# Hash attention with a squared-ReLU feed-forward block: the layout of the first pair's loads, and the parts in which the next chunk's x is loaded

## The chip, the cores and the metric

The kernel runs on one core of one Trainium2 chip. The metric is device microseconds (us) of one execution on that core. The core has a matrix engine (TensorE, PE in the profile; its weight loads are shown apart as PEld), a vector engine (VectorE, DVE), a scalar engine (ScalarE, ACT), GpSimd (POOL) and SyncE (SP). SP, ACT and POOL also issue DMA transfers, each in its own program order; sixteen DMA engines carry them out.

## The reference

Attention over 4 x 8 heads of 768 tokens with 64 features. Six sign bits of a projection give each query and each key a bucket, and a query attends only to keys of its own bucket. The result, 3072 tokens by 512, goes through a feed-forward block with a squared ReLU.

```
q_bits = (einsum('bhsd,dk->bhsk', q, proj) > 0)      # the same for k
mask = q_bucket[:, :, :, None] == k_bucket[:, :, None, :]
scores = where(mask, q @ k.T / sqrt(D), -1e9)
attn = softmax(scores) @ v                           # (4, 8, 768, 64)
x = attn.transpose(0, 2, 1, 3).reshape(3072, 512)
h = x @ w_in                                         # (3072, 2048)
out = (maximum(h, 0) ** 2) @ w_out                   # (3072, 512)
```

## The kernel before, in words

The work of every engine is written out by hand: inside `tc.manual_schedule()` each engine, and each queue of DMA issues, runs its instructions in the order in which the program names them. An instruction that waits holds back all that stands behind it on its engine.

**Attention** (lines 598 to 693, 0 to about 331 us) goes over 16 pairs of heads. For pairs 1 to 15 `load_pair` brings q and k in blocks that VectorE can transpose (`features`). The first pair has a path of its own. `load_first` (L267) loads q and k with six consecutive tokens on one partition, so each partition takes one run of 1536 B per head; one head goes through SP's queue and one through ACT's. `keep_busy(6)` (L329) puts six products of no use on PE while the loads are under way. `first_features(w, r)` (L306) turns three blocks of 128 tokens: per block and head, a product of the loaded 128 x 64 block with the identity gives 64 x 128 in PSUM (L314). The result is copied to `feat`: for q (w = 0) with a strided copy that puts the tokens in their order again, on ScalarE for r = 0 and on VectorE for r = 1 (L319); for k (w = 1) in the order in which it lies, on VectorE (L324). The values of the first pair are loaded with the same six tokens on a partition (L298), so that keys and values agree; later pairs load them in rows of 256 B (L300). Then come the hash products (L352), the signs (L362 on ScalarE, L376 and L380 on VectorE), the scores (L402) and their exponentials (L419). The attention result goes to a DRAM tensor, `x_all`, features by tokens (L503).

**The feed-forward block** (lines 1217 to 1252) goes over three chunks of 1024 tokens. For each chunk there is a stage of hidden products and then `project(i)` (L1059), which makes the output by seven products of blocks, k = 0 to 6, each of them split into seven again. One of these, `product` (L708), runs seven `add` steps of eight PE instructions each on L717, with factors of w_out ("leaf") that ACT's queue loads ahead. In the middle of its program stands `hook` (L1135). Its first instruction is a subtraction on VectorE, `minus(y21, y21, t2)`; the result is the moving operand `t4` of the last `add` of the same product. So the last eight PE instructions of each k wait for that subtraction. After it come `inner_sums(k + 1)`, the sums for the next product.

While chunk 0 is projected, each of k = 0 to 3 begins with `factor_units(k)` (L838). It builds factors of w_in that the next chunk needs: two loads through POOL's queue (L842, 256 KB each), four sums on VectorE (L516 to L519), and four stores through POOL's queue (L851), two of which wait for the sums. Its tiles `h` come from a ring of five buffers.

`load_x(i)` (L557) loads chunk i of `x_all`, 2 MB, through POOL's queue into one tile of four feature blocks. For the next chunk it is called after product k = 0 (L1155). The first reader is `sum_x` on VectorE after product k = 3 (L1157).

The main function is one long function; here is what the diff touches:

Of the kernel before, what the change touches and what calls it, by code (L numbers as in the profile page):

```python
# [8 lines left out]
FP32 = mybir.dt.float32  # L9
# [25 lines left out]
def kernel(  # L35
# [17 lines left out]
    P = 128  # L53
# [212 lines left out]

    def load_first():  # L267


        for src, name in ((q, "q_nat"), (k, "k_nat")):  # L270
            t = p_qk.tile([P, 2, SB, D], FP32, name=name)
            for h, queue in enumerate((nc.sync, nc.scalar)):
                queue.dma_start(
                    out=t[:, h], in_=src[0, h].rearrange("(p t) d -> p t d", t=SB)
                )
            nat[0, name] = t
        for h, queue in enumerate((nc.sync, nc.scalar)):
            queue.dma_start(out=projs[h * D:(h + 1) * D, 0:NBITS], in_=proj)
# [15 lines left out]
    def load_values(pr):  # L294
        b, j = divmod(pr, PB)
        t = p_v.tile([P, 2, SB * D], FP32, name="v_nat")
        if pr == 0:
            nc.sync.dma_start(out=t, in_=v[0, 0:2].rearrange("h (p t) d -> p h (t d)", t=SB))  # L298
        else:
            nc.sync.dma_start(  # L300
                out=t.rearrange("p h (t d) -> p (h t) d", d=D),
                in_=v[b, 2 * j:2 * j + 2].rearrange("h (t p) d -> p (h t) d", t=SB),
            )
        nat[pr, "v_nat"] = t

    def first_features(w, r):  # L306

        if r == 0:
            feat[0, w] = p_f.tile([P, S], FP32, name=f"feat{w}")
        tp = turn("tp")[:, 0]  # L310
        for i in range(SB // 2):
            t = r * (SB // 2) + i
            for h in range(2):
                nc.tensor.matmul(  # L314
                    out=tp[h * D:(h + 1) * D, i * P:(i + 1) * P],
                    lhsT=nat[0, ("q_nat", "k_nat")[w]][:, h, t], rhs=ident, start=True, stop=True,
                )
        if w == 0:
            (nc.vector.tensor_copy if r else nc.scalar.copy)(  # L319
                out=feat[0, w].rearrange("f (p t) -> f t p", t=SB)[:, r * (SB // 2):(r + 1) * (SB // 2)],  # L320
                in_=tp[:, 0:HS].rearrange("f (t p) -> f t p", p=P),
            )
        else:
            nc.vector.tensor_copy(out=feat[0, w][:, r * HS:(r + 1) * HS], in_=tp[:, 0:HS])  # L324

    busy = const.tile([P, 512], BF16, name="busy")
    void = ps_o.tile([P, 1024], FP32, name="xo")
# [1 line left out]
    def keep_busy(n, w=512):  # L329

        for _ in range(n):
            nc.tensor.matmul(  # L332
                out=void[:, 0:w], lhsT=busy[:, 0:P], rhs=busy[:, 0:w], start=True, stop=True
            )
# [186 lines left out]
    def minus(out, in0, in1):  # L521
        nc.vector.tensor_tensor(out=out, in0=in0, in1=in1, op=ALU.subtract)  # L522
# [31 lines left out]

    xs = {}

    def load_x(i):  # L557

        x = p_c.tile([P, NFT, NCH], FP32, name="x")
        nc.gpsimd.dma_start(out=x, in_=x_all[:, :, i * NCH:(i + 1) * NCH])  # L560
        xs[i] = x, [p_c.tile([P, 2, NCH // 2], FP32, name=f"t_x{n}") for n in range(3)]

    w_unit = {}

# [33 lines left out]
    with tc.manual_schedule():  # L598
        nc.vector.memset(busy, 1.0)
        nc.vector.memset(projs, 0.0)  # L600
        load_first()
        keep_busy(6)
        make_identity(nc, ident)
        constants()
        load_pair(1)
# [2 lines left out]
            load_weight(i)  # L608
        first_features(0, 0)
        first_features(0, 1)  # L610
        first_features(1, 0)
        hash_bits(0, void.rearrange("p (h c) -> p h c", h=2), (0,))
        signs(0, 0)
# [445 lines left out]
        def project(i):  # L1059

            V, W, U, X = (p_y.tile([P, 4, QN], FP32, name=f"sum{n}") for n in range(4))
            outs = {}

            def out_block(ih, jh, n):

                row, col = n // 2, n % 2
                if (ih, jh, row) not in outs:
                    outs[ih, jh, row] = [p_y.tile([P, HN], FP32, name="o", bufs=NOUT), 0]
                o = outs[ih, jh, row]
                return o[0][:, col * QN:(col + 1) * QN]  # L1070

            def close(ih, jh, n):
                o = outs[ih, jh, n // 2]
                o[1] += 1
                if (i, ih, jh, n // 2) == (NCHUNK - 1, 1, 0, 1):

                    if o[1] == 2:
                        for col in (1, 0):
                            put_last(n - n % 2 + col, o[0][:, col * QN:(col + 1) * QN])
                elif o[1] == 2:  # L1080
                    put_out(i, ih, jh, n // 2, o[0])

            def first_(n, one, two):
                if two is None:
                    nc.scalar.copy(out=block(V, n), in_=one)
                else:
                    add_to(block(V, n), one, two)

            def seventh(n, one, two):
                add_to(block(W, n), block(V, n), whole(one, two))  # L1090

            def fifth(n, one, two):
                if two is None:
                    nc.scalar.copy(out=block(U, n), in_=one)
                else:
                    add_to(block(U, n), one, two)

            def third(n, one, two):
                add_to(block(X, n), block(U, n), whole(one, two))
                add_to(block(X, n), block(X, n), block(V, n))  # L1100

            def second(n, one, two):
                add_to(out_block(0, 0, n), block(V, n), whole(one, two))
                close(0, 0, n)

            def sixth(n, one, two):
                t = whole(one, two)
                add_to(out_block(0, 1, n), block(X, n), t)
                close(0, 1, n)
                add_to(block(W, n), block(W, n), t)  # L1110
                add_to(out_block(1, 1, n), block(W, n), block(U, n))
                close(1, 1, n)

            def fourth(n, one, two):
                add_to(out_block(1, 0, n), block(W, n), whole(one, two))
                close(1, 0, n)

            more = i + 1 < NCHUNK
            uses = first_, seventh, fifth, third, second, sixth, fourth
            for k in range(7):  # L1120
                b = OUTER[k][1]
                t1, t2 = tens.pop(k)
                if i == 0 and k < NQ:
                    factor_units(k)
                if k == 6 and more:
                    load_inner(i + 1, 0)
                at = lambda m, k=k: lambda n: leaves[k, m][:, n]
                bt = {
                    "11": lambda n: b[:, n, 0:QN], "21": lambda n: b[:, NQ + n, 0:QN],
                    "22": lambda n: b[:, NQ + n, QN:HN], "t1": lambda n: t1[:, n],  # L1130
                    "t2": lambda n: t2[:, n], "t3": lambda n: b[:, n, QN:HN],
                    "t4": lambda n: b[:, NQ + n, 0:QN],
                }

                def hook():  # L1135
                    y21 = b[:, NQ:NR, 0:QN]
                    minus(y21, y21, t2)
                    if k + 1 < 7 and k not in (1, 3):
                        inner_sums(k + 1)
                    if k == 6 and more:  # L1140
                        sums_inner(i + 1)

                counted = []

                def a_with_load(m, k=k):
                    load_leaf(7 * k + len(counted) + NLEAF - 2)
                    counted.append(m)
                    return at(m)

                use = uses[k]  # L1150
                product(
                    NQ, QN, a_with_load, bt, lambda *p: use(0, *p), lambda *p: use(1, *p),
                    lambda p: use(2, p, None), lambda *p: use(3, *p), hook,
                )
                if k == 0 and i + 1 < NCHUNK:  # L1155
                    load_x(i + 1)
                if k in (3, 4) and i + 1 < NCHUNK:  # L1157
                    sum_x(i + 1, 2 * k - 5)
                    sum_x(i + 1, 2 * k - 4)
                if k == 5 and i + 1 == NCHUNK:  # L1160
                    guard()
                if k == 0:

                    for h in range(2):
                        at_h = slice(h * NQ, (h + 1) * NQ)
                        minus(b11[:, at_h], b22[:, at_h], b_t[:, at_h])
                    inner_sums(2)
                if k == 2:

                    for h in range(2):  # L1170
                        at_h = slice(h * NQ, (h + 1) * NQ)
                        minus(b_t[:, at_h], b21[:, at_h], b11[:, at_h])
                    inner_sums(4)
# [315 lines left out]
```

## Time and profile before

| what | value |
|---|---|
| median of 3 runs | 880.36 us (879.87 to 880.45) |
| the profiled execution's own time | 880.36 us |
| its span in the profile | 878.5 us |
| PE busy | 865.6 us, 99% of the span |
| VectorE busy | 760.8 us, 87% |
| ScalarE busy | 391.7 us, 45% |
| POOL busy | 106.9 us, 12% |
| granted TensorE clock, mean | 0.997 |
| x loads (L560) | 3 of 2 MB, median 11.9 us from issue to landing |

The profile is one execution. The span runs from the first to the last instruction, and 1.9 us of the time lie outside it. Busy times count an engine's own instructions; a DMA is counted with the queue that issued it. The chain of work that ended last is followed back from the last instruction: 96% of it is PE. A timeline shows the instructions of an engine in order, "x8" being eight of one kind merged; square brackets hold the idle time before them and what ended it, as far as the profile can tell. "issue" there means that the profile found no releaser.

### The profile page before, as it was taken

The numbers are of one execution on the slowest core, as the hardware profiler recorded it, in microseconds if no ns is written. First come the engines' busy times: TensorE is split into PE (matmuls) and PEld (weight loads), VectorE is DVE, ScalarE is ACT, GpSimd is POOL, SyncE is SP. The second block draws the span as 40 slices with busy tenths as digits, with TensorE's granted clock in tenths as the row PEclk, the third lists the DMA queues.
The fourth block names the chain that finished last, engine by engine and source line by source line (L and its number), as shares of the span: only waits on it lengthen the run. The fifth ranks groups of instructions, "written<-read, shape, count | busy, mean of one in ns | idle before, by whom it ended". The sixth has DMA issues, their size and how long they took to land.

```text
span 878.5 us, 12193 instructions
## 1 busy us (share of the span) xinstructions
PE 865.6 (99%) x4372; PEld 521.1 (59%) x4372; DVE 760.8 (87%) x1100; ACT 391.7 (45%) x672; POOL 106.9 (12%) x172
## 2 busy tenths in 40 slices
PE   8999999999999999999999999999999999999996
PEld 4444444444444444444688865556888755568885
DVE  5999999999999998888779968888889788888875
ACT  6988888888888852222211123332111233321110
POOL 2000000000000000554231011111000211110002
PEclk9999999999999999999999999999999999999998
DMA  9676987899888636999897764536857744455565
GB/s 195 119 150 127 240 164 148 183 257 220 178 183 217 161 108 213 297 263 287 295 342 249 179 159 171 168 117 224 287 147 189 169 162 156 127 167 152 160 171 109
DMA packets 220291, 167.09 MB, mean 190 GB/s; under 512 B 159840, under 2 KB 177504, under 8 KB 220224
## 3 DMA queue, kind: packets, MB, share of 16 engines
q1 hardware_dynamic: 186592, 87.19, 41.3%
q0 software_dynamic: 12528, 41.30, 15.1%
q10 hardware_dynamic: 21104, 37.76, 14.2%
q8 instruction: 36, 0.59, 0.3%
q14 instruction: 31, 0.25, 0.1%
HBM read 124.52 MB, written 41.68 MB: 189 GB/s over the span
## 4 chain that ended last, share of the span: by engine, by line
PE 96%; DVE 2%; ACT 1%; issue 0%; DVEq 0%; ACTq 0%
PE acc L717 40%; PE st L402 17%; PE acc L936 16%; PE xo L444 14%; PE acc L889 6%; PE hash L352 2%; PE tot L461 1%; DVE total L434 1%; ACT bits L362 1%; PE tp L314 0%; ACT e L419 0%; PE xo L332 0%; PE xo L483 0%; DVE x_t L499 0%; DVE recs L493 0%
## 5 line engine op out<-in xcount | busy, mean ns | idle before, releaser
L419 ACT ACTIVATE e<-st 128x1024 f32<-128x1024 f32 x192 | 145.1, 810 | 44.9 <-PE st L402 41.1
L402 PE MATMUL st<-feat,feat 64*128 64x512 f32 (+1 forms) x768 | 150.4, 483 | 0.0
L444 PE MATMUL xo<-e,v_nat 128*64 128x512 f32 (+1 forms) x768 | 134.8, 492 | 0.0
L717 PE MATMUL acc<-b,leaf 128*128 128x256 f32 x600 | 133.4, 379 | 0.9 <-issue 0.9
L717 PEld LDWEIGHTS acc<-b,leaf 128*128 128x128 f32 x600 | 113.8, 190 | 17.6 <-issue 2.3
L434 DVE TENSOR_TENSOR total<-total,e 128x1536 f32<-128x1536 f32 x64 | 112.4, 1756 | 8.2 <-ACT e L419 3.6
L444 PEld LDWEIGHTS xo<-e,v_nat 128*64 128x64 f32 x768 | 51.3, 136 | 82.1 <-issue 74.0
L936 PE MATMUL acc<-t_x,w_unit 128*128 128x512 f32 x192 | 90.2, 592 | 0.0
L402 PEld LDWEIGHTS st<-feat,feat 64*128 64x128 f32 x768 | 66.0, 188 | 32.7 <-issue 23.4
L717 PE MATMUL acc<-t,leaf 128*128 128x256 f32 x336 | 76.2, 380 | 0.0
L362 ACT ACTIVATE bits<-hash,lifts 32x384 bf16<-32x384 f32 x120 | 68.7, 573 | 2.3 <-PE hash L352 0.4
L717 PEld LDWEIGHTS acc<-t,leaf 128*128 128x128 f32 x336 | 63.7, 190 | 9.1 <-DVE t L522 0.5
L801 DVE SCALAR_TENSOR_TENSOR b<-h 128x512 f32<-128x512 f32 x96 | 65.7, 691 | 3.0
L402 PE MATMUL st<-bits,bits 64*128 64x256 bf16 (+1 forms) x384 | 63.0, 325 | 1.7 <-ACT e L419 1.3
L936 PE MATMUL acc<-x,w_unit 128*128 128x512 f32 x128 | 60.2, 592 | 0.0
L717 PE MATMUL acc<-x,w_unit 128*128 128x512 f32 x128 | 56.5, 593 | 0.0
L717 PE MATMUL acc<-b_t,leaf 128*128 128x256 f32 x240 | 53.8, 379 | 0.0
L936 PEld LDWEIGHTS acc<-t_x,w_unit 128*128 128x128 f32 x192 | 36.5, 190 | 28.9 <-issue 26.8
L724 ACT COPY two<-acc 128x256 f32<-128x256 f32 (+1 forms) x29 | 12.5, 432 | 87.7 <-PE acc L717 72.2
L724 ACT COPY one<-acc 128x256 f32<-128x256 f32 (+1 forms) x29 | 12.5, 432 | 85.6 <-PE acc L717 52.1
L717 PEld LDWEIGHTS acc<-b_t,leaf 128*128 128x128 f32 x240 | 45.5, 190 | 6.2
L402 PEld LDWEIGHTS <-bits 64*128 64x128 bf16 x384 | 23.6, 93 | 42.5 <-issue 38.3
(160 smaller groups left out, 1169.7 us busy)
## 6 DMA issues: line engine op xcount, KB each, us to landing
leaf<-w_out ACTq DMA_DIRECT2D x142, 256.0 KB, 3.1
w_unit<-w_in SPq DMA_DIRECT2D x16, 640.0 KB, 4.0
raw<-in_moe_w_in_dram SPq DMA_DIRECT2D x16, 512.0 KB, 5.5
raw<-in_moe_w_out_dram SPq DMA_DIRECT2D x16, 512.0 KB, 4.5
w_unit<-w_in SPq DMA_DIRECT2D x8, 896.0 KB, 7.7
w_out<-sums POOLq DMA_DIRECT2D x16, 448.0 KB, 6.8
sum<-w_in SPq DMA_DIRECT2D x16, 448.0 KB, 4.9
v_nat<-in_v_dram SPq DMA_DIRECT2D x16, 384.0 KB, 4.4
```

The source lines that it names most:

```text
L352: nc.tensor.matmul(out=banks[g * NR_B:(g + 1) * NR_B, h, 0:HS], lhsT=projs[rows], rhs=feat[pr, w][rows, c * HS:(c + 1) * HS], start=True, ...
L362: nc.scalar.activation(out=t[h * D:h * D + NR_B, c * HS:(c + 1) * HS], in_=hashed[pr, w][at, h, 0:HS], func=ACTF.Sign, scale=HUGE, bias=li ...
L402: nc.tensor.matmul(out=st[:, h, 0:hi - lo], lhsT=src[pr, 1][rows, key], rhs=src[pr, 0][rows, lo:hi], start=first, stop=not first,)
L419: nc.scalar.activation(out=e[:, :, lo:hi], in_=sts[i][:, :, 0:hi - lo], func=ACTF.Exp, scale=scale)
L434: nc.vector.tensor_tensor(out=totals[pr], in0=totals[pr], in1=weights[pr, kt][:, :, 0:S], op=ALU.add)
L444: nc.tensor.matmul(out=xo[h * D:(h + 1) * D, lo:hi], lhsT=nat[pr, "v_nat"][:, h, kt * D:(kt + 1) * D], rhs=weights[pr, kt][:, h, lo:hi], s ...
L461: nc.tensor.matmul(out=tot[g * 32:(g + 1) * 32, 0:HS], lhsT=ones, rhs=totals[pr][:, h, c * HS:(c + 1) * HS], start=True, stop=True,)
L717: nc.tensor.matmul(out=acc[to], lhsT=a(i), rhs=b(i), start=first and i == 0, stop=last and i == n - 1, skip_group_check=True,)
L724: nc.scalar.copy(out=t, in_=acc[of])
L801: nc.vector.scalar_tensor_tensor(out=out, in0=h, scalar=0.0, in1=h, op0=ALU.max, op1=ALU.mult)
L889: nc.tensor.matmul(out=out, lhsT=w[:, a], rhs=b, start=start, stop=stop, skip_group_check=True)
L936: nc.tensor.matmul(out=acc[to], lhsT=w[:, PLACE[a], f], rhs=bt[b](f), start=first and f == 0, stop=last and f == NFT // 2 - 1, skip_group_ ...
```

## The change

Two separate edits, at the two ends of the kernel's program.

The first pair's path: q, k and v of pair 0 are loaded with token t x 128 + p on partition p, in rows of 256 B. `first_features` turns a block of 128 tokens and both heads with one 128 x 128 transposing product. All of its copies to `feat` run without a stride; both halves of q are copied by ScalarE. Eight products of no use stand ahead of q's blocks, and two more between q's blocks and k's.

The next chunk's x: `load_x` takes a range of feature blocks. Block 0 is loaded in the hook of product k = 0, block 1 after that product, block 2 in the hook of k = 1 and block 3 after it; each is 512 KB.

```diff
-            t = p_qk.tile([P, 2, SB, D], FP32, name=name)
+            t = p_qk.tile([P, SB, 2, D], FP32, name=name)
             for h, queue in enumerate((nc.sync, nc.scalar)):
                 queue.dma_start(
-                    out=t[:, h], in_=src[0, h].rearrange("(p t) d -> p t d", t=SB)
+                    out=t[:, :, h], in_=src[0, h].rearrange("(t p) d -> p t d", t=SB)
                 )
...
-        if pr == 0:
-            nc.sync.dma_start(out=t, in_=v[0, 0:2].rearrange("h (p t) d -> p h (t d)", t=SB))
-        else:
-            nc.sync.dma_start(
-                out=t.rearrange("p h (t d) -> p (h t) d", d=D),
-                in_=v[b, 2 * j:2 * j + 2].rearrange("h (t p) d -> p (h t) d", t=SB),
-            )
+        nc.sync.dma_start(
+            out=t.rearrange("p h (t d) -> p (h t) d", d=D),
+            in_=v[b, 2 * j:2 * j + 2].rearrange("h (t p) d -> p (h t) d", t=SB),
+        )
...
-            for h in range(2):
-                nc.tensor.matmul(
-                    out=tp[h * D:(h + 1) * D, i * P:(i + 1) * P],
-                    lhsT=nat[0, ("q_nat", "k_nat")[w]][:, h, t], rhs=ident, start=True, stop=True,
-                )
+            nc.tensor.transpose(
+                out=tp[:, i * P:(i + 1) * P],
+                in_=nat[0, ("q_nat", "k_nat")[w]][:, t].rearrange("p h d -> p (h d)"),
+                identity=ident,
+            )
+        out = feat[0, w][:, r * HS:(r + 1) * HS]
         if w == 0:
-            (nc.vector.tensor_copy if r else nc.scalar.copy)(
-                out=feat[0, w].rearrange("f (p t) -> f t p", t=SB)[:, r * (SB // 2):(r + 1) * (SB // 2)],
-                in_=tp[:, 0:HS].rearrange("f (t p) -> f t p", p=P),
-            )
+            nc.scalar.copy(out=out, in_=tp[:, 0:HS])
         else:
-            nc.vector.tensor_copy(out=feat[0, w][:, r * HS:(r + 1) * HS], in_=tp[:, 0:HS])
+            nc.vector.tensor_copy(out=out, in_=tp[:, 0:HS])
...
-    def load_x(i):
-
-        x = p_c.tile([P, NFT, NCH], FP32, name="x")
-        nc.gpsimd.dma_start(out=x, in_=x_all[:, :, i * NCH:(i + 1) * NCH])
-        xs[i] = x, [p_c.tile([P, 2, NCH // 2], FP32, name=f"t_x{n}") for n in range(3)]
+    def load_x(i, n=slice(0, NFT)):
+
+        if i not in xs:
+            x = p_c.tile([P, NFT, NCH], FP32, name="x")
+            xs[i] = x, [p_c.tile([P, 2, NCH // 2], FP32, name=f"t_x{n}") for n in range(3)]
+        nc.gpsimd.dma_start(out=xs[i][0][:, n], in_=x_all[:, n, i * NCH:(i + 1) * NCH])
...
-        keep_busy(6)
+        keep_busy(8)
...
         first_features(0, 1)
+        keep_busy(2)
         first_features(1, 0)
...
                     minus(y21, y21, t2)
+                    if k < 2 and more:
+                        load_x(i + 1, slice(2 * k, 2 * k + 1))
...
-                if k == 0 and i + 1 < NCHUNK:
-                    load_x(i + 1)
+                if k < 2 and i + 1 < NCHUNK:
+                    load_x(i + 1, slice(2 * k + 1, 2 * k + 2))
```

## The prediction

> **What bounds the kernel.** I read the share of each engine first, then the busy time by stretches, then the chain of waits in the stretches that the diff touches, then the timelines of VectorE and POOL there.
>
> ```profile
> PE 865.6 (99%) x4372; PEld 521.1 (59%) x4372; DVE 760.8 (87%) x1100; ACT 391.7 (45%) x672; POOL 106.9 (12%) x172
> ...
> 0.00:33.00 33.00, 29.54 (x218) 15.09 (x222) 21.42 (x55) 23.55 (x34) 4.73 (x19) 1.00 0.97 184
> 442.00:454.00 12.00, 11.29 (x53) 9.65 (x52) 10.60 (x16) 1.49 (x4) 3.79 (x6) 1.00 1.01 376
> 466.00:478.00 12.00, 11.77 (x55) 10.08 (x54) 11.79 (x16) 1.49 (x4) 2.79 (x4) 1.00 0.78 254
> 607.00:692.00 85.00, 85.00 (x394) 74.50 (x393) 76.62 (x110) 11.72 (x32) 8.04 (x13) 1.00 0.70 207
> ```
>
> (Columns after the length: PE, PEld, DVE, ACT, POOL busy with counts, granted clock, DMA share, GB/s.) PE bounds everything. The edits can gain only where PE is idle: 3.5 us in the first 33 us, 0.71 and 0.23 us in the projection of chunk 0. In the projection of chunk 1 (607 to 692) PE has no gap, so loading x in parts gains nothing there; x for chunk 2 is issued at 615.8 and its first reader (t_x, L522) runs near 656, so a later landing costs nothing either.
>
> The chain of waits between 425 and 480:
>
> ```profile
> 450.65 0.71 issue
> 451.37 24.41 PE acc L717 x112
> 475.78 0.23 issue
> ```
>
> "issue" is a wait whose releaser the view did not find. VectorE's and POOL's timelines name it:
>
> ```profile
> 446.15 1.22 DVE L522 TENSOR_TENSOR b_t<-b_t 128x1024 f32<-128x1024 f32 x1
> 448.57 0.42 DVE L516 TENSOR_TENSOR h<-h 128x256 f32<-128x256 f32 x1 [1.21 <-DMA h<-w_in]
> 450.05 1.22 DVE L522 TENSOR_TENSOR b<-b,t 128x1024 f32<-128x1024 f32 x1
> 458.15 0.43 DVE L516 TENSOR_TENSOR h<-h 128x256 f32<-128x256 f32 x1 [4.17 <-DMA h<-w_in]
> 474.69 1.22 DVE L522 TENSOR_TENSOR b<-b,t 128x1024 f32<-128x1024 f32 x1
> ...
> 434.70 0.95 POOL L560 DMA_DIRECT2D x<-x_all  x1
> 435.47 1.28 POOL L842 DMA_DIRECT2D h<-w_in  x2
> 449.97 1.41 POOL L851 DMA_DIRECT2D w_in<-h  x2 [0.43 <-DVE h L518]
> 451.10 0.84 POOL L842 DMA_DIRECT2D h<-w_in  x1
> ```
>
> The subtraction of k = 1 (450.05) ends at 451.27, 0.6 us after PE could have gone on at 450.65: PE's 0.71. It is late because VectorE waited 1.21 us for the loads of `factor_units(1)`, issued on POOL just behind the 2 MB of x. The subtraction of k = 3 (474.69) ends at 475.91, PE's 0.23: VectorE has been busy without a break since 458.15, where it waited 4.17 us for the loads of `factor_units(2)`.
>
> **Part 1, x in parts.** POOL's instructions run in order and none of the x loads waits for PE's progress inside a product, so "in the hook" and "after the product" are the same moment: blocks 0 and 1 go out together where x goes out now, blocks 2 and 3 together behind the stores of `factor_units(1)`. It is two halves, not four quarters.
>
> First half. Between 434 and 447 us the DMA view shows POOL's queue moving 3.12 MB (240 GB/s) beside 1.36 MB of leaves, with the DMA engines full. These 3.1 MB are two stores of 256 KB (issued 433.57), x, and two loads of 256 KB; VectorE starts on them at 448.57, so 15.0 us after the first issue, 13 at 240 GB/s and 2 of latency. With half of x it is 2.1 MB: 8.7 + 2 = 10.7, landing at 444.3. VectorE then goes on directly at 447.35 (446.15 + 1.22), 1.2 us earlier; the subtraction of k = 1 ends at 450.05, before PE needs it. **PE's 0.71 us go.**
>
> Second half. The two stores that wait for the sums are issued 1.24 us earlier, at 448.73. Then come blocks 2 and 3 and, behind them, the loads of `factor_units(2)`. That is again 2.1 MB and 10.7 us: VectorE could start at 459.4 instead of 458.15. Before, only these stores and loads were on the queue, and the second load was issued late (453.57). Between 444 and 450 POOL's queue would stand nearly empty, which before it did not, and that is lost. From 458.15 to 475.91 VectorE is busy throughout, and PE's step in k = 3 hangs on the end of it; so what VectorE starts late, PE ends late, whatever was gained at k = 1. Cost: 459.4 - 458.15 = +1.2 us net, with PE's two waits, 0.94 us, turning into one of 0.94 + 1.2 at k = 3. The leaves' queue has caught up by 450 (before, it had not), so POOL's share should be a bit better than 240: at 275 GB/s it is 7.6 + 2, 458.4, +0.2. I take +0.9, nearer to the slower since its row is the same mix of transfers. Bounds: -0.94, both waits gone (landing by 457.2), and +2.9 (2.1 MB at 200 GB/s, landing at 461). The subtraction of k = 2 has cover: it ends 2.7 us after VectorE starts, PE needs it at 462.8. More DMA issues: 6 x about 0.6 us on POOL over two chunks, 12% busy, hidden. The readers of x at k = 3 come near 480; blocks 2 and 3 land before 459.
>
> **Part 2, the start.**
>
> ```profile
> 4.15 2.83 PE L314 MATMUL tp<-ident,q_nat 128*64 128x128 f32 x24
> 6.77 0.98 PE L314 MATMUL tp<-ident,k_nat 128*64 128x128 f32 x12
> 7.98 0.85 PE L352 MATMUL xo<-feat,projs 64*32 64x384 f32 x8 [0.23 <-issue]
> ...
> L314 PE MATMUL tp<-ident,q_nat x24: 421/421/476, 4.2 to 6.6; 128*64 128x128 f32 x24
> L314 PE MATMUL tp<-ident,k_nat x24: 272/273/421, 6.8 to 9.8; 128*64 128x128 f32 x24
> L1044 PE MATMUL acc<-ident,o x4: 273/300/329, 870.5 to 871.0; 128*128 128x128 f32 x4
> ```
>
> Min/median/max tell that the same product takes 421 ns up to about 6.9 us and 272 after it, and a pair of them comes every 0.21, then every 0.11 us: PE works at half pace until then, though the granted clock reads 1.00. The new transposes are one instruction each (L1044, four blocks, x4), and I give each the cadence of a pair. PE's list up to the hash of q, on the chain of waits throughout: q's blocks start two idle products (0.42 each) later, 4.15 + 0.85 = 5.0; six transposes x 0.21 = 1.3, to 6.3 (24 products, 2.6 us, before); two idle products, to 7.1; three of k at 0.11 to 0.16, to 7.5. The hash starts at 7.5 instead of 7.98. Its feat is ready: ScalarE's copies of 384 columns cost about 0.48 (370 ns for 256, 586 for 512), against 0.85 with the stride, the second ending near 7.0. VectorE loses one copy of 0.85, and k's second three transposes take 0.4 instead of 0.81. The hash of k, the signs and the first exponential (11.83) follow: **-0.45 us**. Bounds: 0 (the transposes at twice the cadence that I gave) and -0.7.
>
> Smaller rows are six times as many. Pairs' values in 256 B rows (L300) land after 4.1 to 5.3 us, the first pair's in 1536 B rows (L298) after 4.7: by the landing no difference. q lands 2.8 to 3.0 us after issue (0.77), so near 3.8; up to 5.0 there are 1.2 us of cover, for k (5.1, used at 7.1) 2.0. Beyond that, each us costs one. Queued behind on SP: pair 1's q and k (used at 14.15), v of pair 0 (18.8) and the first weight piece (landing near 14.1, used by VectorE at 17.5), all with over 2 us.
>
> The Trainium skill speaks against the new transposes: by "TensorE: Matmul & The Clock Gate", Part 4 (PE-mode transpose), transposing products do not count as work for the gate that doubles PE's pace; this trace has none near its start, and so cannot tell. By that rule the start would lose the 1.1 to 1.6 us of the first rival below in place of gaining.
>
> **Sum**, against the profiled execution (880.36, which is also the median): -0.45 + 0.9 = +0.45, so **880.8**.
>
> **Rivals.**
> 1. *PE stays at half pace longer* (slower). PE had worked from 1.48 to 6.9 before its pace doubled. If 6 transposes in a row break that count, half pace lasts past 10 us. Then three transposes (0.33), q's hash (0.85) and k's (0.42) on the chain take twice: +1.6, less what VectorE's and ScalarE's steps hide, at least +1.1. From -0.45 to about +1.0; with +0.9, 882.3 (881.8 to 883.5). For it: the doubling came after 5.4 us of nothing but products. Against: six transposes are only 1.3 us. Chance 0.2.
> 2. *Both waits of the projection go.* If POOL's queue moves the second half at 320 GB/s or over, VectorE starts by 457.3 (448.73 + 6.6 + 2): -0.85 to -0.94, in all 879.0 to 879.1. For it: 1.05 MB less stand ahead at 447. Against: the DMA share is 1.01 in 442 to 454. Chance 0.25.
> 3. *The second half comes much later*, 461 or after, or q's 256 B rows land over 1.2 us later: 882 to 883. Chance 0.1.
> The forecast, 880.8 (880.0 to 881.6): 0.45.
>
> **Chances.** A measurement of this kernel can tell about 0.2%, 1.8 us, from no change. Slower than that (over 882.1): most of rival 1 and of rival 3, 0.19. Faster (under 878.6): 0.03. Same 0.78. Range 879.0 to 882.6: it leaves out the ends of rivals 1, 2 and 3, some 2 in 10.
>
> **What would show it.** PE's wait at k = 1 gone; one wait of about 2 us at k = 3 with VectorE starting L516 of k = 2 near 459; if there are none, rival 2. The hash of q at 7.5 and the first exponential at 11.4. Rows of L314's successor for k over 400 ns, and the hash after 8: rival 1. A wait of q's transposes for a DMA: rival 3. Any change in 33 to 430 or 515 to 878 us beyond a shift would refute the reading that only these two places count.

## The result, and the profile after

The changed kernel takes **883.4 us** (882.48 to 884.14, 6 runs), the kernel before 880.16 (878.87 to 881.27, 6 runs). The ratio is 1.0036, 95% interval [1.0023, 1.0049]: 3.2 us slower. The profiled execution took 882.77 us, 2.41 more than the one before.

The page's busy times, then the busy time by stretches (columns as in the prediction):

```profile
PE 865.2 (98%) x4340; PEld 519.2 (59%) x4340; DVE 760.1 (86%) x1099; ACT 391.8 (44%) x673; POOL 109.8 (12%) x178
```

```profile
0.00:33.00 33.00, 29.29 (x192) 13.24 (x192) 20.95 (x55) 23.95 (x36) 4.73 (x19) 1.00 1.07 179
442.00:454.00 12.00, 12.00 (x57) 10.58 (x56) 10.58 (x16) 1.47 (x4) 4.96 (x8) 1.00 0.92 311
454.00:466.00 12.00, 11.38 (x54) 9.72 (x53) 5.45 (x8) 1.86 (x5) 3.91 (x6) 1.00 0.94 335
466.00:478.00 12.00, 9.60 (x45) 8.11 (x43) 11.93 (x14) 1.49 (x4) 2.45 (x4) 1.00 0.80 254
607.00:692.00 85.00, 85.00 (x391) 73.88 (x390) 76.74 (x111) 12.27 (x33) 9.40 (x16) 1.00 0.68 200
```

PE does the same work but for the start, where it has 32 instructions fewer, and the projection of chunk 1 (607 to 692) still has no gap. In the projection of chunk 0 the gap of 442 to 454 is gone (12.00 of 12.00), and larger ones stand in the next two stretches. The chain of waits between 425 and 520 gives their sizes:

```profile
424.69 37.97 PE acc L713 x168
462.66 0.61 issue
463.27 12.32 PE acc L713 x56
475.60 2.74 issue
478.33 38.23 PE acc L713 x176
```

The waits are 0.61 at k = 2 and 2.74 at k = 3, 3.35 us in place of 0.71 + 0.23 = 0.94. The difference, 2.41, is the whole difference of the two profiled executions. VectorE's timeline, then POOL's, show how they come about:

```profile
447.20 0.42 DVE L510 TENSOR_TENSOR h<-h 128x256 f32<-128x256 f32 x1
448.67 1.22 DVE L516 TENSOR_TENSOR b<-b,t 128x1024 f32<-128x1024 f32 x1
...
460.49 0.43 DVE L510 TENSOR_TENSOR h<-h 128x256 f32<-128x256 f32 x1 [7.73 <-DMA h<-w_in]
461.96 1.22 DVE L516 TENSOR_TENSOR b_t<-b_t,t 128x1024 f32<-128x1024 f32 x1
...
477.02 1.22 DVE L516 TENSOR_TENSOR b<-b,t 128x1024 f32<-128x1024 f32 x1
```

```profile
433.50 1.41 POOL L847 DMA_DIRECT2D w_in<-h  x2 [5.83 <-DVE h L512]
434.63 1.39 POOL L556 DMA_DIRECT2D x<-x_all  x2
435.70 1.38 POOL L838 DMA_DIRECT2D h<-w_in  x2
...
448.58 1.40 POOL L847 DMA_DIRECT2D w_in<-h  x2 [2.30 <-DVE h L512]
449.71 1.39 POOL L556 DMA_DIRECT2D x<-x_all  x2
450.79 1.38 POOL L838 DMA_DIRECT2D h<-w_in  x2
```

POOL issues x in two pairs: two halves, as read from the diff. Behind the first half VectorE starts on the loads of `factor_units(1)` at 447.20 without a wait, so the subtraction of k = 1 (448.67) is in time. Behind the second half it waits 7.73 us and starts at 460.49, where before it was 458.15. From there it is busy until the subtraction of k = 3 (477.02, before 474.69: 2.33 later), and PE waits for that.

The start, in PE's timeline:

```profile
4.87 1.38 PE L309 MATMUL tp<-ident,q_nat 128*128 128x128 f32 x6
6.08 0.59 PE L326 MATMUL xo<-busy 128*128 128x512 bf16 x2
7.21 0.55 PE L309 MATMUL tp<-ident,k_nat 128*128 128x128 f32 x3 [0.54 <-DMA k_nat<-in_k_dram]
7.69 0.85 PE L346 MATMUL xo<-feat,projs 64*32 64x384 f32 x8
```

The hash of q comes at 7.69 in place of 7.98, although PE now waits 0.54 us for k, the later load of which landed 5.9 us after its issue (3.9 before). The first exponential runs at 11.53 in place of 11.83; at 424 us 0.08 of this lead is left.

### The profile page after: what moved, and what is told of

Same layout as the page of the kernel before. It is cut to its first block, busy times and chain, and to the rows that moved or that the text cites. A ratio compares the mean times of both kernels' runs of the same rounds, so it can differ in the third digit from the quotient of the medians.

```text
span 881.0 us, 12143 instructions
## 1 busy us (share of the span) xinstructions
PE 865.2 (98%) x4340; PEld 519.2 (59%) x4340; DVE 760.1 (86%) x1099; ACT 391.8 (44%) x673; POOL 109.8 (12%) x178
## 4 chain that ended last, share of the span: by engine, by line
PE 95%; DVE 2%; ACT 1%; DMA 1%; issue 1%; ACTq 0%; DVEq 0%
PE acc L713 40%; PE st L396 17%; PE acc L932 16%; PE xo L438 14%; PE acc L885 5%; PE hash L346 2%; PE tot L455 1%; DVE total L428 1%; DMA k_nat<-in_k_dram 1%; ACT bits L356 1%; ACT e L413 0%; PE xo L477 0%; DVE x_t L493 0%; PE tp L309 0%; DVE recs L487 0%
```

## The experiments

Theory A: the second half of x, ahead of the loads of `factor_units(2)` on POOL's queue, makes them late, and VectorE and then PE with them. Rivals: the start costs the time; the moment of issue counts and not the bytes ahead; the DMA engines are full in any case, whatever the order. The kernel before had medians of 879.8 to 880.5 on the chips used; each ratio is against it on the same chip.

### The two parts alone

e1: the kernel before with the diff's hunks in `load_x`, `hook` and the call after the product. e2: the rest of the diff.

> The kernel before with x in four parts as in the change, and the start as before. Theory A (the second half of x stands ahead of the loads of factor_units(2) on POOL's queue, and VectorE starts their sums late): PE's wait at k = 1 gone, waits of about 0.6 us at k = 2 and 2.7 us at k = 3, 2.4 us over before in the profile, VectorE's first sum of k = 2 near 460.8 instead of 458.15. Rival B (the smaller rows of the first pair keep the DMA engines behind and cost something later too): under 1.5 us over before here, the rest in the start alone.

> The change's start, with x loaded at once as before. Theory A: 0.3 us under before up to the end of attention, with PE's two waits of 0.71 and 0.23 us as before; 0.0 to 0.3 us under before in all. Rival B: 1 us or more over before.

The parts alone: **884.47** (884.23 to 884.72), 1.005 [1.0036, 1.0063]. The start alone: **879.91**, 1.0001 [0.9992, 1.001]. So the parts make the change slower, and the start makes no difference that can be measured. In e1 VectorE starts at 460.96, and PE's waits are 1.59 and 2.74, 3.39 more than before where theory A had about 2.4 in all. The time grew by 4.4. More than the waits shows in PE's timeline and in the stretches of 2 us behind the second wait (the third number from the end is the granted clock):

```profile
478.82 7.11 PE L718 MATMUL acc<-b,leaf 128*128 128x256 f32 x24 [2.74 <-issue]
```

```profile
478.00:480.00 2.00, 1.18 (x6) 1.08 (x7) 1.93 (x5) 0.00 (x0) 0.82 (x2) 1.00 0.82 291
480.00:482.00 2.00, 2.00 (x7) 1.61 (x6) 1.90 (x5) 0.00 (x0) 0.00 (x0) 0.55 0.28 92
482.00:484.00 2.00, 2.00 (x7) 1.62 (x6) 1.93 (x5) 0.00 (x0) 0.00 (x0) 0.60 0.00 0
484.00:486.00 2.00, 2.00 (x11) 1.74 (x11) 1.67 (x3) 0.37 (x1) 0.00 (x0) 1.00 0.26 52
```

In 480 to 484 the granted clock is 0.55 to 0.60, and PE does 7 instructions in 2 us where it else does 11. The 24 instructions take 7.11 us; in the changed kernel's profile, where the clock stays at 1.00, the same 24 take 5.42. This is a second cost that no theory had, 1.7 us: after waits the clock falls, here for 3 to 4 us. (Waits and clock come to 5.1 us; the profiled execution of e1 began 0.6 us ahead of the one before, with its first exponential at 11.25 against 11.83.)

### Where x stands on the queue

e3, against before: all of x behind product k = 1. e4: all of x between the loads and the stores of `factor_units(1)`. e5: all of x on SP's queue.

```diff
# e3
-                if k == 0 and i + 1 < NCHUNK:
+                if k == 1 and i + 1 < NCHUNK:
# e4
-        def factor_units(n):
+        def factor_units(n, then=None):
...
+            if then:
+                then()
...
+                    factor_units(k, (lambda: load_x(1)) if k == 1 else None)
...
-                if k == 0 and i + 1 < NCHUNK:
+                if k == 0 and 0 < i < NCHUNK - 1:
# e5
-        nc.gpsimd.dma_start(out=x, in_=x_all[:, :, i * NCH:(i + 1) * NCH])
+        (nc.sync if i == 1 else nc.gpsimd).dma_start(
+            out=x, in_=x_all[:, :, i * NCH:(i + 1) * NCH]
+        )
```

> The kernel before with the whole of x issued after product k = 1 instead of k = 0 (in both projections). Theory A: the loads of factor_units(2) stand behind 2 MB instead of 0 (before) and 1 MB (the change). Two stores, x and two loads are 3.1 MB, 15 us as in the k = 1 of the kernel before, from about 448.7: VectorE starts the sums of k = 2 near 463.7, so 5.5 us over before. The wait at k = 1 is gone. Rival C (what counts is the number of parts, or how they share the engines, not what stands ahead of the loads): no more than 1 us over before.

> The kernel before with the whole of x for chunk 1 issued on POOL between the loads and the stores of factor_units(1), so behind the loads that VectorE needs next and well ahead of those of factor_units(2). Theory A: both of PE's waits go, VectorE starts the sums of k = 2 at or before 457.2: 0.9 us under before. Rival C: x just delays the next loads, as in the change; 0 to 2 us over before.

> The kernel before with the whole of x for chunk 1 issued on SP's queue, at the same place after product k = 0. Theory A (what stands ahead on POOL's queue decides): the loads of factor_units(1) and (2) no longer stand behind x, VectorE does not wait at k = 1, PE's 0.71 goes, and the 0.23 too if the sums of k = 2 start by 457.2; 0.7 to 0.9 us under before. Rival D (the sixteen DMA engines' total decides, whatever the queue): the loads of factor_units(1) land as late as before, 0 to 2 us over before.

e3: **886.49**, 1.0071 [1.0056, 1.0086]; VectorE's start of k = 2 moves to 464.80, PE waits 4.74 and 1.05, and the clock falls behind the first wait (0.50 in 468 to 470, 0.67 in 470 to 472). With 2 MB ahead in place of 1 VectorE starts 3.8 us later than in e1 and 4.3 later than in the change. e4: 879.81, 0.9999 [0.999, 1.0008]. The wait at k = 1 goes, VectorE starts k = 2 at 457.49, and 0.35 us of wait stay at k = 3; of the expected gain of 0.94 us the waits show 0.59, and the time none that can be told from noise. e5: 878.3, 0.9984 [0.9975, 0.9993]; VectorE starts k = 2 at 456.17, with 0.18 us of wait left.

### Only the order of the second half

e7 is e1, and e9 the changed kernel, with blocks 2 and 3 issued behind the two loads of `factor_units(2)` in place of ahead of them. The bytes and the moment of issue stay, to about 1 us.

```diff
-        def factor_units(n):
+        def factor_units(n, then=None):
...
+            if then:
+                then()
...
-                    factor_units(k)
+                    factor_units(k, (lambda: [load_x(1, slice(n, n + 1)) for n in (2, 3)]) if k == 2 else None)
...
-                    if k < 2 and more:
+                    if k < 2 - (i == 0) and more:
...
-                if k < 2 and i + 1 < NCHUNK:
+                if k < 2 - (i == 0) and i + 1 < NCHUNK:
```

> x in four parts, blocks 0 and 1 at k = 0 as in the change, blocks 2 and 3 on POOL between the loads and the stores of factor_units(2); the start as before. Theory A: the loads of factor_units(2) have only two stores of 256 KB ahead of them and land near 454.5 to 456, VectorE starts the sums of k = 2 before 457.2, both of PE's waits go: 0.9 us under before, so 5 us under the same parts in the change's order (e1). Rival D (the bytes in this stretch decide, not their order): within 1.5 us of e1.

> The changed kernel with this one order turned: blocks 2 and 3 of x behind the loads of factor_units(2) instead of ahead of them. Theory A: no wait of PE in the projection of chunk 0, 0.9 to 1.2 us under before, 4 to 4.5 under the change. Rival D: within 1.5 us of the change.

e7: **878.65**, 0.9986 [0.9977, 0.9995], 5.8 us under e1. e9: **878.6** (878.37 to 879.6), 0.9988 [0.9979, 0.9997], 4.8 us under the change. Each of these pairs ran on two chips; by the ratios to before, the differences are 5.6 and 4.2 us. POOL's and VectorE's timelines of e9:

```profile
448.38 1.40 POOL L849 DMA_DIRECT2D w_in<-h  x2 [2.55 <-DVE h L512]
449.51 1.39 POOL L838 DMA_DIRECT2D h<-w_in  x2
450.59 1.37 POOL L556 DMA_DIRECT2D x<-x_all  x2
```

```profile
455.67 0.43 DVE L510 TENSOR_TENSOR h<-h 128x256 f32<-128x256 f32 x1 [3.10 <-DMA h<-w_in]
```

The same instructions, two pairs of them exchanged: VectorE starts 4.8 us earlier (455.67 against 460.49), and PE has no wait left in this projection (0.22 us in e7). Profiles of one and the same projection differ by less: before, e2 and e6, which share it, start at 458.15, 456.94 and 458.37. This settles the cause: it is the order on the queue. Had the bytes in this stretch decided, whatever their order (rival D), e7 and e9 would have been within 1.5 us of e1 and the change.

### The dose

e12 is the changed kernel with one block moved to the first half: three out after k = 0, one after k = 1.

```diff
-                    if k < 2 and more:
-                        load_x(i + 1, slice(2 * k, 2 * k + 1))
+                    if k < 1 and more:
+                        load_x(i + 1, slice(0, 1))
...
-                    load_x(i + 1, slice(2 * k + 1, 2 * k + 2))
+                    load_x(i + 1, slice(2 * k + 1, 3 + k))
```

> The changed kernel with one block of x (0.5 MB) moved from the second half to the first: three blocks go out after product k = 0, one after k = 1. A test of dose. Theory A (the loads of factor_units(2) are late by the bytes that stand ahead of them on POOL's queue): with 0 blocks ahead VectorE's sums of k = 2 start at 458.15 (before), with 2 at 460.49 (the change), with 4 at 464.80 (x after product 1). Taking 0.5 MB away gains 1.1 us by the first pair and 2.2 us by the second (per block), so 458.3 to 459.4; PE waits 1.1 to 2.2 us in all in place of 3.35, and the time is 0.5 to 0.6 us better still if the clock no longer falls: 880.3 to 882.2 against 883.4. The first half costs nothing: with three blocks the loads of factor_units(1) land near 446.5, before VectorE is free at 447.2. Rival T (what counts is when the stores and blocks are issued, and that POOL's queue stands empty before it, not how many bytes): 460.5 and 883.4 as in the change.

881.54 us, 1.0015 [1.0006, 1.0025]. VectorE starts k = 2 at 458.91, 1.58 us earlier than in the change, for 0.5 MB less. That fits theory A and not rival T (the moment of issue), whose 460.5 it misses, but it is no clean dose: POOL issues the second load of `factor_units(2)` only at 453.13, after 1.88 us of waiting for a store, and the first half's last load lands at 447.3, in the change at 445.3. The cleaner comparisons are e9 against the change for the order, and e3 against e1 for the bytes. The first half did cost VectorE something here, a wait of 0.50 us, but PE none. The chain of waits has one wait left, 2.22 us, and the clock falls behind it:

```profile
450.13 24.41 PE acc L713 x112
474.54 2.22 issue
476.76 39.81 PE acc L713 x176
```

```profile
476.00:478.00 2.00, 1.24 (x3) 1.09 (x4) 1.93 (x5) 0.00 (x0) 0.77 (x2) 0.64 0.86 273
478.00:480.00 2.00, 2.00 (x6) 1.55 (x6) 1.86 (x6) 0.00 (x0) 0.00 (x0) 0.51 0.32 123
480.00:482.00 2.00, 2.00 (x11) 1.77 (x10) 1.97 (x4) 0.00 (x0) 0.00 (x0) 1.00 0.00 0
```

Its eleven times fall into two groups, 880.09 to 881.54 (6) and 882.56 to 883.16 (5). The profiled execution (882.9) is of the second, and has the fall. The mean granted clocks of the first group are 0.996 to 0.998, those of the second 0.995 and 0.996.

### The clock behind the wait

e10 is e1 with products of no use where PE waits: 6 ahead of the last `add` of k = 2, 12 ahead of that of k = 3. Each is two PE instructions in the profile. All of e1's own work stays.

```diff
-        def product(n, w, at, bt, c11, c12, c21, c22, hook=None):
+        def product(n, w, at, bt, c11, c12, c21, c22, hook=None, fill=0):
...
+            if fill:
+                spare = ps_t.tile([P, 512], FP32, name="acc3")[:, 0:P]
+                for _ in range(fill):
+                    nc.tensor.matmul(out=spare, lhsT=ident, rhs=ident, start=True, stop=True)
...
+                    {(0, 2): 6, (0, 3): 12}.get((i, k), 0),
```

> e1 (four parts in the change's order, the start as before) with products of no use, identity times identity, that PE runs where it would wait: 6 ahead of the last add of k = 2 (about 1.3 of 1.6 us) and 12 ahead of that of k = 3 (about 2.6 of 2.7 us). Theory K (after these waits PE works at half pace for about 3.5 us, which costs 1.6 us more than the waits): the granted clock stays 1.00 in 478 to 490, and the kernel is about 1.5 us faster than e1, 2.8 to 3.4 over before. Rival (the lower clock in that profile is an accident of that execution): same as e1 or slower, 4.4 over before.

882.6 us (882.07 to 883.42), 1.0036 [1.0023, 1.005]: 1.9 us under e1, which was on another chip, and 1.2 by the ratios; the two intervals overlap, so the size is rough. The clock is plain. PE's timeline and the stretch in which e1 had 0.86:

```profile
475.15 2.84 PE L746 MATMUL acc<-ident 128*128 128x128 f32 x24
478.03 5.42 PE L718 MATMUL acc<-b,leaf 128*128 128x256 f32 x24
```

```profile
478.00:490.00 12.00, 11.97 (x56) 10.58 (x57) 11.66 (x19) 1.49 (x4) 0.03 (x1) 1.00 0.44 133
```

With PE busy while it waits, the clock stays at 1.00, and the 24 instructions take 5.42 us in place of 7.11.

### The rows of the start, and x on SP again

e6 is before with only the rows of 256 B (q, k and v of pair 0); e11 is the change with chunk 1's four parts on SP, and e13 the start with all of x on SP, by the same edit as in e5.

> Before, with only the layout of the first pair's loads changed (rows of 256 B; products, copies and idle products in number as before; the copies of q run without a stride). The change's profile shows k landing 5.9 us after its issue, against 3.5 to 3.9 before, and PE waiting 0.54 us for it. Theory R (the small rows do this): k lands near 7.1 again, PE waits for it 0.2 to 0.5 us, the hash of q comes at 8.2 to 8.5 in place of 7.98 and the first exponential between 11.5 and 12.2; the time is 880.0 to 881.0. Theory S (that profile was chance, or it was the two added idle products): k lands near 5.1, no wait, the hash at 7.9, the first exponential at 11.0 to 11.8, the time 879.3 to 880.2. The moment at which PE's pace doubles has varied by up to 2.8 us from run to run, so the landing decides and not the time.

> The changed kernel with chunk 1's x, in its four parts, issued by SP in place of POOL. Theory A: nothing stands ahead of the loads of factor_units on POOL's queue, both waits of the projection go, and the time is that of before with x on SP (878.3) within 0.5 us: 877.8 to 878.8. Rival B (the start's edit is worth its forecast 0.45 us): 877.4 to 877.9 more often than not. If the DMA engines and not the queue's order are the limit: VectorE's sums of k = 2 start after 458 and the time is over 880.

e6: 880.69, 1.0006 [0.9997, 1.0015]; k landed 5.6 us after its issue and PE waited 0.42 us for it, as theory R has it. The profiles of all runs bear it out as a tendency: with rows of 256 B the later load of k landed after 5.1 to 5.9 us in all eight, with rows of 1536 B after 3.8 to 4.1 in six and 5.1 and 5.5 in two (e1 and e4), and e4 has a wait of 0.41 us for k without the small rows. So the rows make k later as a rule, but they are not the only thing that does, and their cost is too small for the time to show. e11: 880.92, 1.0006 [0.9997, 1.0015], 2 us above what theory A gives for it. VectorE does start k = 2 early (456.71), so neither the queue's order nor late sums are the reason: PE waits 0.8 us for a leaf, a wait that the profile of before does not show. To tell whether the start, the four parts or the chip does this, three kernels on one chip:

> The change's start with chunk 1's x whole on SP's queue, beside its two relatives on the same chip: before with x whole on SP, and the change with its four parts on SP (880.92 in its run, where PE waited 0.82 us for a leaf). Theory P (four transfers of 0.5 MB in place of one of 2 MB on SP take the leaves' share): 878.0 to 878.9, at one with before plus x on SP, and the four parts 1.5 us or more above both. Theory S (the start's edit costs 2 us that its own run hid): 880 to 881, at one with the four parts. Theory C (the chip of that run): all three within 0.6 us of each other.

> Before with x whole on SP, again, on the chip of its two relatives. Theories P and S: 0.9984 of before, about 878.3. Theory C: as the other two.

> The change with its four parts of x on SP, again, on the chip of its two relatives. Theory P: 1.5 us or more above both. Theory S: as the start with x whole on SP, and above before with x on SP. Theory C: as the other two.

e13: 880.36, 1.0009 [1.0, 1.0018]. e5 again: 879.09, 0.9992 [0.9983, 1.0001]. e11 again: 880.96, 1.0007 [0.9997, 1.0016]. No theory holds as stated; S comes nearest, with e13 in its 880 to 881 and 0.6 us from the four parts. It is not the chip alone; the four parts cost at most 0.6 us over the whole; e13 lies 1.3 us above e5 (S had 2), and its waits name leaves:

```profile
PE acc L714 <- DMA leaf<-w_out: 1.3, 2, 0.7
PE tp L309 <- DMA k_nat<-in_k_dram: 0.4, 1, 0.4
```

In the profiles PE's waits for leaves are 0.0 and 0.3 us in e5's two runs, 0.8 and 0.8 in e11's, 1.3 in e13, and none in before, the change, e7 and e9. So x on SP takes the wait from POOL's queue and gives some of it back at the leaves. Why more with the new start, some 420 us earlier, is **open**; the start alone (e2) and in e9 against e7 (878.6 and 878.65) shows no such loss.

## Why the prediction was wrong

The forecast was 880.8, the range 879.0 to 882.6; the result is 883.4. The place and the chain were right, and the sizes wrong. Of the 2.6 us between forecast and result, 1.5 are the second half of x, 0.45 the start, and 0.6 lie between the profiled execution and the median.

**The step that failed** is the second half of x: "That is again 2.1 MB and 10.7 us", and from it "Cost: ... I take +0.9". The loads came 11.9 us after the stores' issue at 448.58, where the forecast had 10.7 and 9.6 us, at 240 and 275 GB/s; VectorE started 2.34 us later than before, and the waits grew by 2.41 us. The forecast took 15.0 us for 3.1 MB, set 2 us of it down as latency and scaled the other 13 with the bytes, so that 1.05 MB less would save 4.3 us. It saved 3.1, and in both halves: in the first, the two stores were issued at 433.50 and the last load landed at 445.3, after 11.8 us, where the forecast had 444.3. The same two halves took 10.9 and 12.9 us in e1 and 11.8 and 12.3 in e10: all more than 10.7, and the second never less than the first.

The reason that it gave for the faster end was "The leaves' queue has caught up by 450 ..., so POOL's share should be a bit better than 240". The DMA views show the opposite (q0 is POOL's queue, q10 that of the leaves; packets, MB, share of the engines). First the row of before that the forecast took its rate from, 434 to 447, then the change from 448.6 to 460.5:

```profile
q0 software_dynamic: 834, 3.12, 62.0%
q10 hardware_dynamic: 740, 1.36, 33.9%
```

```profile
q0 software_dynamic: 609, 2.10, 47.1%
q10 hardware_dynamic: 970, 1.77, 43.8%
```

The leaves moved 149 GB/s here, against 105 in before's row. POOL's 2.10 MB in 11.9 us are 176 GB/s with the latency in it; before's 3.1 MB in 15.0 us, taken the same way, are 210. Much of the lag is early: in the first 3 us in which POOL's queue moved data, 449.6 to 452.6, it moved 0.36 MB and the leaves 0.52; in before's first 3 us, 435.6 to 438.6, it was 0.72 and 0.25. That the leaves took the share is read from these views; a kernel without them was not tried, so this part is argued and not shown. Shown are the landing and, by e9, that the order on the queue makes it late.

The other steps:

- **The first half of x: right in the result, by cover.** PE's 0.71 us at k = 1 went, and VectorE went on at 447.20 (forecast 447.35). The loads were 1 us later than forecast here too, but VectorE was not free before 447.20.
- **"What VectorE starts late, PE ends late": right**, 2.34 us there, 2.41 here. The cover of k = 2's subtraction ("PE needs it at 462.8") did not hold at VectorE's later start: PE waited 0.61 us there, which moved part of the wait ahead and cost nothing more.
- **A term that was missing: the clock behind the wait.** The forecast had a wait of about 2 us and gave it no price beyond its length. In the change's profile the clock does not fall; the two of its six runs with a mean granted clock of 0.997 took 882.48 and 882.77, the four with 0.995 and 0.996 took 883.4 to 884.14. This may explain the median's 0.6 us over the profiled execution, but it is an inference, and e1 does not bear it out: its five times lie within 0.5 us at mean clocks of 0.995 to 0.997. That the clock falls behind such waits is shown in e1, e3 and e12; in e10, where they are filled, the profile has no fall. The Trainium skill, "TensorE: Matmul & The Clock Gate", Part 1 (The HAM clock gate), puts the return to half pace after an idle window of about 3.4 us. The runs here differ: in e12 a single wait of 2.22 us was enough in the profiled execution, and by the two groups of times in about half of its runs.
- **The start: -0.45 forecast, nothing measurable.** -0.30 us at the first exponential, 0.08 left at 424 us. That six transposes take about 0.21 us each, 1.3 in all, was right (4.87 to 6.08). The 2.0 us of cover "for k (5.1, used at 7.1)" were wrong: k landed 2 us later, and the cover was negative by 0.54. The forecast took the landing of later pairs' values, "by the landing no difference"; e6 and the other profiles show later landings with the small rows. The baseline was one profile, too, and one in which PE's pace doubled as late as in any: over all profiles the mean of the first exponential is 11.45 us with the loads, products and copies of before (eight profiles, 10.81 to 11.85) and 11.22 with those of the change (seven, 11.01 to 11.53), a gain of some 0.2 us.
- **Rival 1 (transposes hold PE at half pace): did not occur.** The pace doubled at 5.93 us in the change's profile, within its six transposes, and at 5.51, also within them, in e2; in none of the seven profiles with the new start did it come after 7.0 us, where rival 1 had "past 10". The rule of the Trainium skill ("TensorE: Matmul & The Clock Gate", Part 4, PE-mode transpose) that spoke for it does not show in these runs.
- **Rivals 2 and 3.** Rival 2 (both waits go) did not occur in the change; they went only when the order was turned (e9). The second half landed at 460.5, near rival 3's 461, which had 0.1.
- **The range left out its own bounds.** The bound of the second half was +2.9 and that of the start 0: together 883.3. The range ended at 882.6, since the ends of the rivals were cut off; it should have gone to at least 883.3, and with a price for the clock beyond 884.
- "Any change in 33 to 430 or 515 to 878 us beyond a shift" did not occur: each stretch differs by some 0.2 us between the two profiles. The two chances that mattered, same 0.78 and slower 0.19, followed from the mis-sized term.

## What to carry to other kernels

On a queue that works in order, ask of a split transfer not when each part is needed but what small load stands behind it, and whose wait ends last there; here turning two neighbours on POOL's queue was worth 4.2 to 4.8 us and put the change a little under the kernel before (0.9988 [0.9979, 0.9997]). Do not scale the time of a long run of transfers with its bytes alone: a third less took a fifth less time here, beside a busy queue. Give a wait of PE of 2 us or more a second price for the clock behind it (1.7 us in e1), and let the range reach the bounds that the text itself has worked out.

## What the runs showed of the hardware beyond that

- The granted clock, averaged over 2 us, fell to 0.50 to 0.67 for 3 to 4 us behind waits of 2.22 us (e12), 1.59 and then 2.74 (e1) and 4.74 us (e3), and not behind 0.61 and then 2.74 (the change's profile). By the two groups of e12's times it happens in some runs of a program and not in others; one profile of each kernel cannot show that.
- The moment at which PE's pace doubles at the start varies from run to run: 6.98 us in before and 4.15 to 6.98 in six other kernels with the same start, 4.87 to 7.00 in the seven profiles with the new one. First exponentials lay between 10.81 and 11.90 us in all profiles. A gain of 0.3 us read from one profile of the start is within this.
- When the four loads of q and k started together, rows of 256 B made the later load of k land 5.1 to 5.9 us after its issue, against 3.8 to 5.5 with rows of 1536 B, and ACT's load of q 3.7 to 3.9, against 3.0 to 3.3.
